# A gated mix of linear attention and a one-token FFN: gate/up in four batches of eight pieces, and kv times wo on the full TensorE array

## The chip, the cores and the metric

The kernel runs on one core of one Trainium2 chip. The metric is the device time of the whole program in microseconds (us), smaller is better; a version is measured by the median of several executions. The engines of the core are named as in the profile: PE (TensorE, matrix multiply; PEld is its weight load), DVE (VectorE), ACT (ScalarE), POOL (GpSimd) and SP (SyncE, which here only issues transfers).

## The reference

2048 tokens of width 1024 go through two branches that a per-token gate mixes. Branch a is linear attention with 32 heads of width 32. Branch b is a gated FFN (width 3584) that is applied to a single token, the one with the largest router logit; all other tokens pass through unchanged.

```python
x = A_x                                             # 1 x 2048 x 1024, bf16
g = sigmoid((x * gate_w).sum(-1, keepdims=True))
# a: linear attention
q, k, v = heads(x @ wqkv)                           # 32 heads of 32
phi = lambda t: where(t > 0, t + 1, exp(t)) + 1e-6
kv = einsum("bhsd,bhse->bhde", phi(k), v)           # 32 x 32 for each head
z  = einsum("bhsd->bhd", phi(k))
o  = einsum("bhqd,bhde->bhqe", phi(q), kv) / (einsum("bhqd,bhd->bhq", phi(q), z) + 1e-6)
a  = merge(o) @ wo
# b: FFN of the one token with the largest x @ w_r
r = x @ w_r;  i = argmax(r)
y = (silu(x[i] @ w_gate) * (x[i] @ w_up)) @ w_down
b = x;  b[i] += y * sigmoid(r[i])
return g * a + (1 - g) * b
```

## The kernel before

**Three stages.** The tokens are 16 tiles of 128 (t), the width is 8 blocks of 128 (c for the contraction, g for a group of four heads), and the queries are taken in 4 blocks of 512 tokens (j). The first stage makes keys and values tile by tile and sums kv; the second makes the rest of the queries, the denominators and the product of kv and wo; the third multiplies normalised queries with that product and mixes.

*First stage* (loop from L521): for each t, four `unit_KV(t, nb)` of eight 128x512 matmuls each (keys for nb 0 and 1, values for 2 and 3), with ACT and DVE emptying the PSUM bank; one `unit_KVACC(t - 1)` of eight 128x129 matmuls that add to kv (column 129 of each group is z); and some `unit_Q(g, j)`, eight 128x512 matmuls each, `Q_PER_T` of them per tile, j by j and g by g. Work of the FFN is put in between: `ffn_step(4)` at the places in `GU_AFTER`, `down_step` by `DOWN_STEPS`. A PSUM pool of four banks (`ps_work`) serves all these units.

*FFN pieces.* The weights stream through `ffw`, a ring of `FFN_DEPTH` = 9 buffers of 512 KB. `ffn_pieces` fixes the order of the stream: 16 pieces of gate and up for the first half of the hidden width (512 columns each), then, four times, four pieces of the second half (384 columns each) and two pieces of w_down, then the rest of w_down, and last four pieces with wo, ahead of the first of which stands the copy of x to the scratch `xp` and the load of the gate logits. A piece is taken from the front of `inflight` (L490, L500) and the next one is asked for at once (`ffn_prefetch`), all on SP in one order. A gate or up piece is 4 matmuls of an M = 32 stationary operand, one for each column tile (128x32) of the array, so that four run side by side. A w_down piece is two multiply-adds on DVE, 128x1024 each. One PSUM bank (`ps_ffn`) holds gate, then up, then the transposed h (`hps`), which is made at the next step of either kind (`ffn_flush`).

*End of the first stage* (L542 to L559): `unit_Q`, the last `unit_KVACC`, `down_finish` (the FFN row, written into `xp` by a POOL transfer), `gates`, two more `unit_Q`; z is copied to `zc` and kv to `kvbd`. Then the stage's buffers are given back (`ph1.close`, L559), and the second stage's tiles (`m_sb`, `kvT`, `rdp`, `tmpb`) take their place.

*Second stage* (L637 to L650). `den_group(0)`: 16 matmuls on column tiles; ACT adds eps, DVE takes the reciprocal (3.34 us), and SP and POOL transfers spread it to `rdp`. Then the last 15 `unit_Q`. After the first, `unit_kvT` transposes the 32 head blocks with 32 matmuls of 32x32; after those numbered in `M_AFTER` (3, 6, 9, 12) comes a `unit_M(hf, nh)`: 16 matmuls of 32x32 stationary and 512 columns, one for each 32x32 tile of the array, for half of the groups and half of the output columns. Each fills four banks (`four_banks`, three of `ps_den` and `ps_ffn`), which ACT (three) and DVE (one) copy to `m_sb`. From the fifth unit on, `norm_step(1)` broadcasts a reciprocal with a DVE shuffle (`rb`) and multiplies a block of queries on POOL.

*Third stage* (loop from L653): per tile one load of `xt` from `xp`, one ACT scale to `xg`, 16 matmuls 128x512 against `m_sb`, two DVE mixes to `ot`, one store. `den_group(1)` and the other 16 norm steps stand here, `NORM_PER_T` per tile.

**What sets the order.** Tiles, buffers and semaphores are handled by a planner: it takes the program's order as the priority, estimates when each instruction can start, and puts those that it holds ready into each engine's queue; a queue then runs in order. Where `strict[0]` is true, the wrappers `pe`, `dve`, `sp` and `act` tie each instruction to the one before on its engine, so the written order holds. In most of the first stage it is off; in `den_group` and in the loop of the second stage (L640 to L649) it is on. All matmuls and DVE operations go through such a wrapper, which is why most of the profile's lines are L78; the names of the tiles tell them apart.

Of the kernel before, what the change touches and what calls it, by code (L numbers as in the profile page):

```python
# [32 lines left out]
Q_PER_T = {4: 2, 5: 1, 6: 1, 7: 2, 8: 1, 9: 1, 10: 2, 11: 1, 12: 1, 13: 1, 14: 1, 15: 0}  # L33
GU_AFTER = {(6, "end"), (7, 1), (7, "end"), (8, 1), (8, "end"), (9, "end"), (10, "end"), (11, "end")}
M_AFTER = {3: (0, 0), 6: (0, 1), 9: (1, 0), 12: (1, 1)}
DOWN_STEPS = {9: (1, 1, 1, 1), 10: (1, 1, 1, 1), 11: (1, 1, 1, 1), 12: (1, 1, 1, 1, 1), 13: (1, 1, 1, 1), 14: (1, 1, 1, 1), 15: (1, 1, 1)}
FFN_DEPTH = 9
NORM_PER_T = [3, 2, 0, 2, 2, 2, 2, 2, 2, 2, 2, 0, 0, 0, 0, 0]
# [3 lines left out]
def kernel(  # L42
# [103 lines left out]
    nc.scalar.dma_start(out=wrg_rows[8:16, :], in_=gate_w.rearrange("(c p) -> c p", p=P))  # L146
    nc.gpsimd.memset(mzc[:], 0.0)
# [220 lines left out]
    ffw = phq.enter_context(tc.tile_pool(name="ffw", bufs=FFN_DEPTH, side="right"))  # L368
# [75 lines left out]
    def wo_pieces():  # L444
        wo_v = A_wo.rearrange("(hf r c e) n -> hf r e c n", hf=2, r=4, c=4)
        for k in range(4):
            def load(k=k):
                if k == 0:
                    cp = nc.sync.dma_start(out=xp[:], in_=x2d)
                    tc.add_manual_dep(cp.ins, ffn_state["last_ld"].ins.name, NOSYNC, reason="queue order")  # L450
                    ffn_state["last_ld"] = cp
                    gate_logits()
                wt = ffw.tile([P, 2048], BF, tag="ffw")
                for r in range(4):
                    ld = nc.sync.dma_start(out=wt[32 * r : 32 * r + 32, :].rearrange("p (c n) -> p c n", c=2),
                                           in_=wo_v[k // 2, r][:, 2 * (k % 2) : 2 * (k % 2) + 2, :])
                    tc.add_manual_dep(ld.ins, ffn_state["last_ld"].ins.name, NOSYNC, reason="queue order")
                    ffn_state["last_ld"] = ld
                return wt

            yield load, None

    def ffn_pieces():
        gu, dn = gate_up(1), down_rows()
        yield from gate_up(0)
        for _ in range(4):
            yield from islice(gu, 4)
            yield from islice(dn, 2)
        yield from dn
        yield from wo_pieces()  # L470
# [4 lines left out]
    def ffn_prefetch():  # L475
        while len(inflight) < FFN_DEPTH:
            nxt = next(pieces, None)
            if nxt is None:
                return
# [161 lines left out]
    for i in range(len(q_units)):  # L641
        unit_Q(*q_units.popleft())
        if i == 0:
            unit_kvT()
# [63 lines left out]
```

## Time and profile before

| what | value |
|---|---|
| median of 3 executions | 256.62 us (256.43 to 257.25) |
| the profiled execution | 257.25 us |
| its span, first to last instruction | 255.7 us |
| busy: DVE, ACT, POOL | 147.8, 125.7, 47.0 us |
| moved by DMA | 47.72 MB, mean 187 GB/s |
| stage 1, 0 to 166.2 us: PE busy | 162.7 us of 166.2 |
| stage 2, 166.2 to 195.3 us: PE, ACT, DVE busy | 28.7, 24.4, 21.6 us of 29.1 |
| stage 3, 195.3 to 251.9 us: PE, DVE, POOL busy | 56.3, 41.4, 27.9 us of 56.6 |

The span is what the profiler sees of one execution; the time of the execution is 1.55 us longer. The stages' rows come from the view of busy time by windows. The groups that belong to what is changed:

```profile
L78 PE MATMUL ps<-wt,xs_pad 128*32 128x512 bf16 (+1 forms) x128 | 7.5, 355 | 0.0
L78 PE MATMUL pm<-wt,kvT 32*32 32x512 bf16 x64 | 1.7, 384 | 0.0
L78 PE MATMUL pt<-ident,kvbd 32*32 32x32 bf16 x32 | 0.3, 184 | 0.0
L78 ACT CAST m_sb<-pm 128x512 bf16<-128x512 f32 x12 | 6.2, 585 | 0.0
L78 DVE CAST m_sb<-pm 128x512 bf16<-128x512 f32 x4 | 2.7, 681 | 0.0
```

A row has the line, the engine and the operation, the tile written and the tiles read, the sizes and the number of instructions; then the busy time in us and the mean of one in ns; then the idle time of the engine before them. The duration of a single matmul is its latency, longer than the spacing of matmuls that follow each other, since they are pipelined.

### The profile page before, as it was taken

The numbers are of one execution on the slowest core, as the hardware profiler recorded it, in microseconds if no ns is written. First come the engines' busy times: TensorE is split into PE (matmuls) and PEld (weight loads), VectorE is DVE, ScalarE is ACT, GpSimd is POOL, SyncE is SP. The second block draws the span as 40 slices with busy tenths as digits, with TensorE's granted clock in tenths as the row PEclk, the third lists the DMA queues.
The fourth block names the chain that finished last, engine by engine and source line by source line (L and its number), as shares of the span: only waits on it lengthen the run. The fifth ranks groups of instructions, "written<-read, shape, count | busy, mean of one in ns | idle before, by whom it ended". The sixth has DMA issues, their size and how long they took to land.

```text
span 255.7 us, 3936 instructions
## 1 busy us (share of the span) xinstructions
PE 247.7 (97%) x1471; PEld 115.1 (45%) x1498; DVE 147.8 (58%) x243; ACT 125.7 (49%) x200; POOL 47.0 (18%) x94
## 2 busy tenths in 40 slices
PE   7899999999999999999999999999999999999993
PEld 3444455445444444445444444444444444444442
DVE  0046015232246349996799813584888999953442
ACT  2096334556354444645446445468889533333200
POOL 5000001010000000000000000210566779950000
PEclk9999999999999999999999999999999999999999
DMA  6999990009999999878897760030000474454122
GB/s 178 312 336 227 260 329 7 0 19 352 348 341 320 291 275 360 266 229 299 313 489 216 180 151 0 4 123 23 0 1 3 130 223 159 143 187 141 64 82 83
DMA packets 47498, 47.72 MB, mean 187 GB/s; under 512 B 18604, under 2 KB 35380, under 8 KB 47416
## 3 DMA queue, kind: packets, MB, share of 16 engines
q1 hardware_dynamic: 47192, 47.34, 60.6%
q8 instruction: 11, 0.18, 0.3%
q0 software_dynamic: 256, 0.14, 0.2%
q14 instruction: 7, 0.06, 0.1%
q10 hardware_dynamic: 32, 0.00, 0.0%
HBM read 39.34 MB, written 8.40 MB: 187 GB/s over the span
## 4 chain that ended last, share of the span: by engine, by line
PE 95%; DMA 2%; issue 1%; SPq 1%; DVE 0%
PE ps L78 86%; PE kvacc L78 3%; PE first L78 2%; DMA wkv<-in_A_wqkv_dram 2%; PE dps L78 1%; PE rps L78 1%; SPq L78 1%; PE pm L78 1%; PE yps L78 0%; DVE ot L78 0%; PE xs_ps L78 0%; PE hps L78 0%; PE pt L78 0%; PE wps L78 0%
## 5 line engine op out<-in xcount | busy, mean ns | idle before, releaser
L78 PE MATMUL ps<-wkv,xT 128*128 128x512 bf16 x465 | 107.1, 379 | 0.7
L78 PEld LDWEIGHTS <-xT 128*128 128x128 bf16 x512 | 48.8, 98 | 59.1 <-issue 4.5
L78 PE MATMUL ps<-xT,wq 128*128 128x512 bf16 x250 | 57.4, 379 | 0.6 <-issue 0.5
L78 ACT ACTIVATE u<-ps 128x512 f32<-128x512 f32 x60 | 35.9, 598 | 40.4 <-PE ps L78 37.2
L78 PE MATMUL ps<-m_sb,pq_all 128*128 128x512 bf16 (+1 forms) x259 | 55.3, 372 | 0.3
L78 ACT ACTIVATE e<-u 128x512 f32<-128x512 f32 x64 | 40.3, 630 | 2.0
L606 POOL TENSOR_TENSOR pq_all<-pq_all,rb 128x512 bf16<-128x512 bf16 x32 | 36.6, 1169 | 14.4 <-DVE rb L78 14.0
L78 PEld LDWEIGHTS <-pq_all 128*128 128x128 bf16 x264 | 25.8, 98 | 29.8 <-issue 0.4
L78 PEld LDWEIGHTS <-wq 128*128 128x128 bf16 x256 | 24.5, 98 | 30.3 <-issue 1.7
L78 DVE SCALAR_TENSOR_TENSOR pq_all<-ps,e 128x512 bf16<-128x512 f32 x32 | 22.0, 688 | 25.7 <-ACT e L78 25.6
L78 DVE SCALAR_TENSOR_TENSOR yacc<-wt,hcol,yacc 128x1024 f32<-128x1024 bf16 x27 | 34.6, 1281 | 2.2 <-DMA wt<-in_B_w_down_dram 1.7
L78 ACT CAST vt<-ps 128x512 bf16<-128x512 f32 x32 | 18.8, 588 | 34.5 <-PE ps L78 34.5
L78 DVE SCALAR_TENSOR_TENSOR ot<-ps,gate,xg 128x512 bf16<-128x512 f32 (+1 forms) x33 | 24.0, 735 | 15.0 <-PE ps L78 14.0
L78 ACT ACTIVATE xg<-xt,omg 128x1024 f32<-128x1024 bf16 x16 | 18.1, 1146 | 25.8 <-DVE ot L78 25.8
L78 DVE SCALAR_TENSOR_TENSOR pk<-ps,e 128x512 bf16<-128x512 f32 x28 | 19.2, 687 | 19.6 <-ACT e L78 19.6
L78 DVE STREAM_SHUFFLE rb<-rdp 128x512 f32<-128x512 f32 x32 | 22.8, 746 | 0.0
L206 POOL MEMSET vt<- 128x8 bf16 x16 | 1.9, 138 | 108.8 <-PE kvacc L78 108.8
L78 PEld LDWEIGHTS <-pk 128*128 128x128 bf16 x128 | 8.5, 98 | 3.3 <-issue 0.4
L78 PE MATMUL kvacc<-vt,pk 128*128 128x129 bf16 x128 | 9.7, 221 | 0.1
L78 PE MATMUL first<-wkv,xT 128*128 128x512 bf16 x31 | 7.8, 395 | 0.8 <-DMA wkv<-in_A_wqkv_dram 0.6
L78 DVE CAST r_bf<-rps 128x512 bf16<-128x512 f32 x1 | 0.7, 692 | 12.1 <-PE rps L78 12.1
L78 PE MATMUL ps<-wt,xs_pad 128*32 128x512 bf16 (+1 forms) x128 | 7.5, 355 | 0.0
(96 smaller groups left out, 78.6 us busy)
## 6 DMA issues: line engine op xcount, KB each, us to landing
wt<-in_B_w_down_dram SPq DMA_DIRECT2D x14, 512.0 KB, 5.5
wt<-in_B_w_gate_dram SPq DMA_DIRECT2D x8, 512.0 KB, 6.0
wt<-in_B_w_up_dram SPq DMA_DIRECT2D x8, 512.0 KB, 7.2
xt<-xp SPq DMA_DIRECT2D x16, 256.0 KB, 2.7
out_dram<-ot SPq DMA_DIRECT2D x15, 256.0 KB, 2.0
wt<-in_B_w_gate_dram SPq DMA_DIRECT2D x8, 384.0 KB, 5.7
wt<-in_B_w_up_dram SPq DMA_DIRECT2D x8, 384.0 KB, 6.5
wkv<-in_A_wqkv_dram SPq DMA_DIRECT2D x8, 256.0 KB, 5.6
```

Of the source, the lines that this page charges most:

```text
L78: inst = fn(*a, **k)
L206: nc.gpsimd.memset(vt_t[t][:, :, 128:129], 1.0)
L606: nc.gpsimd.tensor_tensor(sl, sl, rb[:], op=ALU.mult)
```

## The change

- **Gate and up.** `GU_AFTER` has four places instead of eight, and eight pieces are taken at each. The stream's order is 16 pieces of the first half, 2 of w_down, 8, 4 of w_down, 8, and the rest of w_down. The number of buffers stays 9; the ring moves from the pool `phq` (which lives until the end of the second stage) to `ph1` (which ends with the first).
- **wo.** It is no longer a part of that stream. After `ph1.close` one 2 MB transfer on SP brings it into a tile of its own. The copy of x to `xp` and the load of the gate logits are issued once the stream has no piece left.
- **kv times wo.** `kvbd` is multiplied with a mask of the head blocks (made by POOL memsets at the start) when it is copied out of PSUM; eight 128x128 transposes go to one bank and one DVE copy makes `kvT`; `unit_M(g)` is two matmuls on the full array, each followed by an ACT copy.
- **Order.** One `unit_Q` more stands at t = 13 and one less after `gates`; one stands between `den_group(0)` and the transposes; 14 are left for the loop, and the eight `unit_M` follow the seventh to the fourteenth. The strict order of `den_group` and of that loop is dropped. A norm step follows each unit of the loop, and `NORM_PER_T` is 2, 0, 0, then 3.

```diff
@@ -30,12 +30,11 @@
 EPS = 1e-6
 LN1EPS = math.log1p(EPS)
 N_WARM = 6
-Q_PER_T = {4: 2, 5: 1, 6: 1, 7: 2, 8: 1, 9: 1, 10: 2, 11: 1, 12: 1, 13: 1, 14: 1, 15: 0}
-GU_AFTER = {(6, "end"), (7, 1), (7, "end"), (8, 1), (8, "end"), (9, "end"), (10, "end"), (11, "end")}
-M_AFTER = {3: (0, 0), 6: (0, 1), 9: (1, 0), 12: (1, 1)}
+Q_PER_T = {4: 2, 5: 1, 6: 1, 7: 2, 8: 1, 9: 1, 10: 2, 11: 1, 12: 1, 13: 2, 14: 1, 15: 0}
+GU_AFTER = {(6, "end"), (8, 1), (9, "end"), (11, "end")}
 DOWN_STEPS = {9: (1, 1, 1, 1), 10: (1, 1, 1, 1), 11: (1, 1, 1, 1), 12: (1, 1, 1, 1, 1), 13: (1, 1, 1, 1), 14: (1, 1, 1, 1), 15: (1, 1, 1)}
 FFN_DEPTH = 9
-NORM_PER_T = [3, 2, 0, 2, 2, 2, 2, 2, 2, 2, 2, 0, 0, 0, 0, 0]
+NORM_PER_T = [2, 0, 0, 3, 3, 3, 3, 3, 3, 3, 3, 3, 3, 3, 3, 3]
 
 
 @with_exitstack
@@ -144,6 +143,10 @@
     make_identity(nc, ident[:])
     nc.scalar.dma_start(out=wrg_rows[0:8, :], in_=B_w_r.rearrange("(c p) -> c p", p=P))
     nc.scalar.dma_start(out=wrg_rows[8:16, :], in_=gate_w.rearrange("(c p) -> c p", p=P))
+    mask_bd = const.tile([P, P], F32)
+    nc.gpsimd.memset(mask_bd[:], 0.0)
+    for i in range(4):
+        nc.gpsimd.memset(mask_bd[32 * i : 32 * i + 32, 32 * i : 32 * i + 32], 1.0)
     nc.gpsimd.memset(mzc[:], 0.0)
     for hh in range(4):
         for g0 in range(4):
@@ -365,7 +368,7 @@
         act.activation(sig[:], xs_ps[:, KC : KC + 1], ACTF.Exp, scale=-1.0)
         dve.tensor_scalar_add(sig[:], sig[:], 1.0)
         dve.reciprocal(sig[:], sig[:])
-    ffw = phq.enter_context(tc.tile_pool(name="ffw", bufs=FFN_DEPTH, side="right"))
+    ffw = ph1.enter_context(tc.tile_pool(name="ffw", bufs=FFN_DEPTH))
     h_bf = [rt.tile([P, 512], BF, name=f"h_bf{i}") for i in range(2)]
     sg_t = [rt.tile([P, 512], F32, name=f"sg{i}") for i in range(2)]
     ffn_state = {}
@@ -441,41 +444,27 @@
 
             yield load, compute
 
-    def wo_pieces():
-        wo_v = A_wo.rearrange("(hf r c e) n -> hf r e c n", hf=2, r=4, c=4)
-        for k in range(4):
-            def load(k=k):
-                if k == 0:
+    def ffn_pieces():
+        gu, dn = gate_up(1), down_rows()
+        yield from gate_up(0)
+        for n in (2, 4):
+            yield from islice(dn, n)
+            yield from islice(gu, 8)
+        yield from dn
+
+    pieces = ffn_pieces()
+    inflight = deque()
+
+    def ffn_prefetch():
+        while len(inflight) < FFN_DEPTH:
+            nxt = next(pieces, None)
+            if nxt is None:
+                if not ffn_state.get("copied"):
+                    ffn_state["copied"] = True
                     cp = nc.sync.dma_start(out=xp[:], in_=x2d)
                     tc.add_manual_dep(cp.ins, ffn_state["last_ld"].ins.name, NOSYNC, reason="queue order")
                     ffn_state["last_ld"] = cp
                     gate_logits()
-                wt = ffw.tile([P, 2048], BF, tag="ffw")
-                for r in range(4):
-                    ld = nc.sync.dma_start(out=wt[32 * r : 32 * r + 32, :].rearrange("p (c n) -> p c n", c=2),
-                                           in_=wo_v[k // 2, r][:, 2 * (k % 2) : 2 * (k % 2) + 2, :])
-                    tc.add_manual_dep(ld.ins, ffn_state["last_ld"].ins.name, NOSYNC, reason="queue order")
-                    ffn_state["last_ld"] = ld
-                return wt
-
-            yield load, None
-
-    def ffn_pieces():
-        gu, dn = gate_up(1), down_rows()
-        yield from gate_up(0)
-        for _ in range(4):
-            yield from islice(gu, 4)
-            yield from islice(dn, 2)
-        yield from dn
-        yield from wo_pieces()
-
-    pieces = ffn_pieces()
-    inflight = deque()
-
-    def ffn_prefetch():
-        while len(inflight) < FFN_DEPTH:
-            nxt = next(pieces, None)
-            if nxt is None:
                 return
             inflight.append((nxt[0](), nxt[1]))
 
@@ -524,7 +513,7 @@
             if nb == 1 and t > 4:
                 unit_KVACC(t - 1)
             if (t, nb) in GU_AFTER:
-                ffn_step(4)
+                ffn_step(8)
             steps = DOWN_STEPS.get(t, ())
             if nb < len(steps):
                 down_step(steps[nb])
@@ -538,12 +527,11 @@
         if t == 5:
             router_part2()
         if (t, "end") in GU_AFTER:
-            ffn_step(4)
+            ffn_step(8)
     unit_Q(*q_units.popleft())
     unit_KVACC(NT - 1)
     down_finish()
     gates()
-    unit_Q(*q_units.popleft())
     unit_Q(*q_units.popleft())
 
     zcol = keep.tile([P, NG], F32)
@@ -555,13 +543,15 @@
     for i in range(3):
         n = 3 if i < 2 else 2
         acc3 = kvacc[i][:, 0 : 129 * n].rearrange("p (g e) -> p g e", e=129)
-        dve.tensor_copy(kvbd[:, 3 * i : 3 * i + n, :], acc3[:, :, 0:128])
+        dve.tensor_tensor(kvbd[:, 3 * i : 3 * i + n, :], acc3[:, :, 0:128],
+                                mask_bd[:].unsqueeze(1).to_broadcast([P, n, P]), op=ALU.mult)
     ph1.close()
 
     pb = ctx.enter_context(tc.tile_pool(name="pb", bufs=1))
     m_sb = pb.tile([P, NG, D], BF)
-    wo = list(inflight)
-    kvT = pb.tile([P, 2, 4, 32], BF)
+    wo = pb.tile([P, NG, D], BF)
+    nc.sync.dma_start(out=wo[:], in_=A_wo.rearrange("(g p) n -> p g n", p=P))
+    kvT = pb.tile([P, NG, P], BF)
     rdp = [pb.tile([P, 512], F32, name=f"rdp{i}") for i in range(2)]
     for r in rdp:
         nc.gpsimd.memset(r[:], 1.0)
@@ -570,7 +560,6 @@
 
     def den_group(pair):
         dps = ps_den.tile([P, 512], F32, tag="d")
-        strict[0] = True
         for g0 in range(4):
             for jj in range(2):
                 for g1 in range(2):
@@ -579,7 +568,6 @@
                     q = 2 * jj + g1
                     pe.matmul(dps[32 * q : 32 * q + 32, :], lhsT=zc[:, g, :], rhs=pq_all[:, g, 512 * j : 512 * j + 512],
                                      start=(g0 == 0), stop=(g0 == 3), tile_position=(0, 32 * q))
-        strict[0] = False
         dn = tmpb.tile([P, 512], F32, tag="dn")
         act.activation(dn[:], dps[:], ACTF.Identity, bias=eps_t[:, 0:1])
         rd = tmpb.tile([P, 512], F32, tag="rd")
@@ -605,48 +593,32 @@
             sl = pq_all[:, g, 512 * j : 512 * j + 512]
             nc.gpsimd.tensor_tensor(sl, sl, rb[:], op=ALU.mult)
 
-    def four_banks(name):
-        banks = [ps_den.tile([P, 512], F32, tag="d", name=f"{name}{r}") for r in range(3)]
-        banks.append(ps_ffn.tile([P, 512], F32, tag="f", name=f"{name}3"))
-        return banks
-
-    def unit_kvT():
-        pt = four_banks("pt")
-        for hf in range(2):
-            for r in range(4):
-                for c in range(4):
-                    pe.matmul(pt[c][32 * r : 32 * r + 32, 32 * hf : 32 * hf + 32],
-                              lhsT=kvbd[32 * c : 32 * c + 32, 4 * hf + r, 32 * c : 32 * c + 32],
-                              rhs=ident[32 * c : 32 * c + 32, 32 * c : 32 * c + 32],
-                              start=True, stop=True, tile_position=(32 * c, 32 * r))
-        for c in range(4):
-            eng = dve.tensor_copy if c % 2 else act.copy
-            eng(kvT[:, :, c, :], pt[c][:, 0:64].rearrange("p (h d) -> p h d", h=2))
-
-    def unit_M(hf, nh):
-        pm = four_banks("pm")
-        for c in range(4):
-            for r in range(4):
-                pe.matmul(pm[r][32 * c : 32 * c + 32, :], lhsT=kvT[32 * r : 32 * r + 32, hf, c, :],
-                          rhs=wo[2 * hf + c // 2][0][32 * r : 32 * r + 32, 1024 * (c % 2) + 512 * nh : 1024 * (c % 2) + 512 * nh + 512],
-                          start=True, stop=True, tile_position=(32 * r, 32 * c))
-        for r in range(4):
-            eng = dve.tensor_copy if r == 3 else act.copy
-            eng(m_sb[:, 4 * hf + r, 512 * nh : 512 * nh + 512], pm[r][:])
+    def unit_M(g):
+        for nh in range(2):
+            ps = ps_den.tile([P, 512], F32, tag="d")
+            pe.matmul(ps[:], lhsT=kvT[:, g, :], rhs=wo[:, g, 512 * nh : 512 * nh + 512], start=True, stop=True)
+            act.copy(m_sb[:, g, 512 * nh : 512 * nh + 512], ps[:])
 
     rdA = den_group(0)
+    unit_Q(*q_units.popleft())
+    pt = ps_den.tile([P, NG, P], BF, tag="d")
+    for g in range(NG):
+        pe.transpose(pt[:, g, :], kvbd[:, g, :], ident[:])
+    dve.tensor_copy(kvT[:], pt[:])
     normalise(rdA, 0)
     normalise(rdA, 1)
-    strict[0] = True
-    for i in range(len(q_units)):
+    g_m = 0
+    nq_done = 0
+    while q_units:
         unit_Q(*q_units.popleft())
-        if i == 0:
-            unit_kvT()
-        if i in M_AFTER:
-            unit_M(*M_AFTER[i])
-        if i >= 4:
-            norm_step(1)
-    strict[0] = False
+        nq_done += 1
+        if g_m < NG and nq_done > 6:
+            unit_M(g_m)
+            g_m += 1
+        norm_step(1)
+    while g_m < NG:
+        unit_M(g_m)
+        g_m += 1
     phq.close()
 
     fin = ctx.enter_context(tc.tile_pool(name="fin", bufs=3))
```

## The prediction

> **What bounds the kernel now.** I read the page from the top: the busy time of each engine and the 40 slices, then the chain that ended last, then the groups, and last the timeline of TensorE (PE) and the SyncE (SP) transfer issues around each place that the change touches.
>
> ```profile
> span 255.7 us, 3936 instructions
> PE 247.7 (97%) x1471; PEld 115.1 (45%) x1498; DVE 147.8 (58%) x243; ACT 125.7 (49%) x200; POOL 47.0 (18%) x94
> PE   7899999999999999999999999999999999999993
> PEclk9999999999999999999999999999999999999999
> PE 95%; DMA 2%; issue 1%; SPq 1%; DVE 0%
> ...
> L78 ACT ACTIVATE u<-ps 128x512 f32<-128x512 f32 x60 | 35.9, 598 | 40.4 <-PE ps L78 37.2
> L78 ACT ACTIVATE e<-u 128x512 f32<-128x512 f32 x64 | 40.3, 630 | 2.0
> ```
>
> PE is busy from the second slice to the last but one, at the full granted clock, and 95% of the chain lies on it. So there is no stage in which another engine sets the pace: each microsecond of PE work put in or taken out, and each wait on PE, should show one for one. All other engines matter only through such waits.
>
> **The prices on PE**, from its timeline (start, busy time, what, how many):
>
> ```profile
> 66.42 1.89 PE L78 MATMUL ps<-xT,wq 128*128 128x512 bf16 x8
> 68.24 1.05 PE L78 MATMUL ps<-wt,xs_pad 128*32 128x512 bf16 x16
> 69.22 3.63 PE L78 MATMUL ps<-wkv,xT 128*128 128x512 bf16 x15
> ...
> 106.81 0.63 PE L78 MATMUL kvacc<-vt,pk 128*128 128x129 bf16 x8
> 107.28 3.62 PE L78 MATMUL ps<-wkv,xT 128*128 128x512 bf16 x16
> 110.74 3.62 PE L78 MATMUL ps<-xT,wq 128*128 128x512 bf16 x16
> ...
> 180.19 0.43 PE L78 MATMUL pm<-wt,kvT 32*32 32x512 bf16 x16
> 180.56 5.35 PE L78 MATMUL ps<-xT,wq 128*128 128x512 bf16 x23
> 185.84 0.43 PE L78 MATMUL pm<-wt,kvT 32*32 32x512 bf16 x16
> 186.21 5.35 PE L78 MATMUL ps<-xT,wq 128*128 128x512 bf16 x24
> ```
>
> Busy times overlap, so only differences of starts are prices. A 128x512 matmul: 16 from 107.28 to 110.74, 3.46/16 = 0.216 us; a unit of eight is 1.73. A gate/up batch of four pieces: 69.22 - 66.42 = 2.80, less one unit, 1.07. Its 16 matmuls run four at a time on column tiles, so the work is 4 x 0.216 = 0.86, and **0.21 us is the price of going into column tiles and back**. The 384-wide batches give the same: 0.86 against 4 x 0.162 = 0.65. One unit_M: 186.21 - 180.56 = 5.65, less 24 matmuls (5.18), 0.47. unit_kvT: from 167.20 to 174.91 stand 32 matmuls (6.91), one unit_M and it; 7.71 - 6.91 - 0.47 = 0.33.
>
> **The change, part by part.**
>
> 1. *kv times wo.* Gone: 4 x 0.47 + 0.33 = 2.21. New: 16 full matmuls of 512 columns, 16 x 0.216 = 3.46, and eight 128x128 transposes. For these the least is the spacing of kvacc (0.47 for eight 128x129, 106.81 to 107.28) and the most that of the transposes at the start, eight from 7.68 to 8.36, 0.68; I take 0.68, the same operation. **+1.93** (bounds +1.72, +1.93). Here a rule speaks against the change. The Trainium skill (TensorE: Matmul & The Clock Gate, Part 3, measured speedup) gives 10.6 times for sixteen 32x32 tiles; as an estimate that is 16 x 0.216/10.6 = 0.33 for a unit_M, where the trace has 0.47 with the switch of modes. By the page the part would cost +2.5; the measured row decides.
>
> 2. *Gate/up in four batches.* The matmuls stay; four pairs of mode switches go: 4 x 0.21, **-0.84**.
>
> 3. *The first batch needs its eighth piece sooner.* Now the first batch eats four pieces at 68.24 and the next four at 73.25. Single issues, and their microseconds from issue to landing, of the seventh and the ninth load:
>
> ```profile
> 60.12 1.29 SPq L382 DMA_DIRECT2D wt<-in_B_w_gate_dram  x1
> 62.81 1.62 SPq L382 DMA_DIRECT2D wt<-in_B_w_up_dram  x1
> ...
> wt<-in_B_w_gate_dram SPq DMA_DIRECT2D x1, 512.0 KB, 9.4
> wt<-in_B_w_up_dram SPq DMA_DIRECT2D x1, 512.0 KB, 9.7
> 118.03 1.28 DVE L78 SCALAR_TENSOR_TENSOR yacc<-wt,hcol,yacc 128x1024 f32<-128x1024 bf16 x1 [1.66 <-DMA wt<-in_B_w_down_dram]
> ```
>
> They land at 69.5 and 72.5, the eighth between them at 71.0. Nothing ahead of 68.24 changes, so the batch starts there, is through seven pieces at 68.24 + 7 x 0.216 = 69.75, and waits **1.25 us**. It costs nothing only if the planner, which puts instructions into each engine's queue by its own estimate of readiness, sets key/value matmuls of token tile 7 before the last piece (then about 0.2 for one more switch: the lower bound). It can: at 92.52 two such matmuls stand between the h transposes and a batch. But the last row, VectorE (DVE) held 1.66 us by a weight piece, shows that it counts on transfers sooner than they land; I take 1.25. Queued behind the waiting matmul is all of PE; ScalarE (ACT) and DVE only have less to do meanwhile. The later batches are fed: the second starts at 71.3 + 14.8 = 86.1 (six units, two kvacc groups, two more units), its last piece lands near 83; the third near 102.5 needs the piece that takes the first down piece's buffer, free about 2.3 us after the h columns (92.69 to 94.97 now), so near 97.5, plus 3.8 to land, 101.3; the fourth has some 4 us. Zero for these.
>
> 4. *ScalarE while wo is multiplied.* Now ACT copies 12 of 16 m_sb parts, DVE 4, spread over 10 units. After, ACT copies all 16 (589 ns each) in the last eight units: 0.60 + 0.63 + 2 x 0.59 = 2.41 us against 8 x 0.216 + 2 x 0.216 = 2.16 on PE. From the end of the first of these units, ACT has the copy of (g 7, left half) done at 8 x 2.41 - 0.59 = 18.7; PE would want it at 7 x 2.16 + 0.43 + 7 x 0.216 = 17.1. Up to **1.6 us** of wait at the first output tile, or before it on the three PSUM buffers. Down to 0.1 if the planner foresees it and runs the right half's seven ready matmuls (1.51) in between. The row at 92.52 speaks for the low end, the row at 118.03 for the high; I take 0.8. The ordering lists of the old loop, which kept two units behind the last unit_M, are gone, so this cover is gone too.
>
> 5. *wo by its own transfer.* It waits on SP until the first stage's buffers are free, about 165.3 (where xt is issued now). A 2048 KB load (wq) took 8.3 us, so it lands by 174; the first unit_M comes after den (0.98), one unit, the transposes and seven units, at 166.2 + 1.0 + 1.7 + 0.7 + 12.1 = 181.7. Zero; without these 8 us of cover, one for one. Behind it on SP stand the xt loads, wanted at 195, and the rdp rows, issued at 171.6. If those land at 175.6 instead of 174.2, the broadcasts hold DVE while PE has four buffers, 5 us of units. The Trainium skill (DMA: Bandwidth & Descriptors, Issuing engines are not separate DMA queues) says that the half issued by GpSimd shares the same 16 DMA engines; by it both halves come later and the sum stays, since the cover is the same. No row here shows the two together. The sixteen 128 KB loads of before, off the path, vanish; the copy of x moves behind seven down pieces, to land near 150 (141 now), wanted at 162.
>
> 6. *Small things.* Five memsets on an idle GpSimd; the mask product in place of a copy, 0.1 us each on DVE, behind zc; the den matmuls lose their fixed order but keep their inputs; three broadcasts per output tile instead of two: now DVE is busy 14.00 of 14 us from 209 to 223 and PE does not stop. Zero.
>
> **Sum**: 1.93 - 0.84 + 1.25 + 0.8 = **+3.1 us**. The profiled execution took 257.25 (span 255.7 and 1.55 around it), so 260.4 like for like; the median shown, 256.62, is 0.63 lower: **259.7**.
>
> **Rivals.** *Both waits hidden* (17%): the planner fills them. Then 1.72 to 1.93, less 0.84, plus 0.2 and 0.1: 1.2 to 1.4, **257.9**. For it the row at 92.52, against it the one at 118.03.
> *The loosened order breaks up the den matmuls* (17%): the 16 run four abreast in 0.98; if the planner lets other matmuls in between, they cost up to 16 x 0.216 = 3.46, +2.5 for one group, **262.2**. Likeliest in the second group, at the first output tile, where part 4 leaves PE waiting and its inputs come one unit at a time. Against it: all 16 stand side by side now, but by that very order.
> *The switches cost more than I read* (7%), so it is faster: the weight loads show 0.42 us of idle at the entry and at the exit of each batch, 0.84 together. If PE really lost that, four batches would give back 3.4, and 1.93 - 3.36 = -1.4 with the waits hidden, **255.2**. It decides from 1.93/4 = 0.48 per batch; the starts say 0.21.
> *It does not do what it says*: a batch is split by the planner. That is the first rival with more switches, 257.9 to 258.5; counted there.
>
> **How the numbers follow.** The forecast has 56%, on its own range 258.7 to 261.2 (part 3 and 4 at either end); 3% is left for no net change. The range goes down past the first rival and up past the den case: 257.4 to 262.4. A measurement of this kernel tells 0.3% (0.77 us) from no change, so "same" is 255.9 to 257.4: the 3% and the low flank of the first rival, 0.09; faster 0.06; slower 0.85.
>
> **What would show it.** Right: four runs of 32 column-tile matmuls, a gap of about 1.2 us on PE near 70 ended by the landing of a gate piece; 16 matmuls into m_sb of 0.216 each; ACT busy without pause in the last 17 us of the query units, and PE waiting on an m_sb copy at the first output tile. Wrong: den matmuls apart from each other; PE waiting on wo or on a DVE broadcast; PE's busy time lower than before; a stall at the third batch.

## The result, and the profile after

The changed kernel takes **265.76 us** (median of 4 runs, 264.72 to 267.13); the kernel before, run beside it, 256.58. The ratio is 1.0356, with a 95% interval of 1.0302 to 1.041: slower by 9.2 us, where 3.1 were forecast, and beyond the range's top of 262.4. The profiled execution took 265.26 us, its span is 263.7: 8.0 more than the span before. From the page of the changed kernel, the rows that answer to those of before:

```profile
span 263.7 us, 3784 instructions
PE 251.4 (95%) x1400; PEld 117.4 (45%) x1426; DVE 145.3 (55%) x238; ACT 126.9 (48%) x202; POOL 47.0 (18%) x99
PE   7899999999689999999989999999999999999994
PEclk9999999999959999999999999999999999999999
PE 84%; DMA 8%; SPq 3%; DVE 3%; issue 1%; ACT 0%; DVEq 0%; POOLq 0%
L77 PE MATMUL ps<-wt,xs_pad 128*32 128x512 bf16 (+1 forms) x128 | 8.0, 368 | 3.4 <-DMA wt<-in_B_w_gate_dram 3.4
```

PE is no longer busy throughout. Slices 11 and 12 show a 6 and an 8, and in slice 12 the granted clock (the share of full speed that TensorE was given) is at 0.5; a lower 8 stands near slice 21. The chain of waits has 8% on transfers and 3% on SP where it had 2% and 1%, and the gate/up group has 3.4 us of idle time ahead of it, ended by gate pieces, where it had none. (The helpers' line is now L77.) So most of the loss sits in one place. The timeline of PE around the first batch of eight (start, busy time, what, how many, and the idle time before):

```profile
67.89 1.05 PE L77 MATMUL ps<-wt,xs_pad 128*32 128x512 bf16 x16
69.20 0.40 PE L77 MATMUL ps<-wt,xs_pad 128*32 128x512 bf16 x4 [0.27 <-DMA wt<-in_B_w_gate_dram]
70.70 0.40 PE L77 MATMUL ps<-wt,xs_pad 128*32 128x512 bf16 x4 [1.10 <-DMA wt<-in_B_w_gate_dram]
72.21 0.62 PE L77 MATMUL ps<-wt,xs_pad 128*32 128x512 bf16 x4 [1.10 <-DMA wt<-in_B_w_gate_dram]
73.72 0.62 PE L77 MATMUL ps<-wt,xs_pad 128*32 128x512 bf16 x4 [0.90 <-DMA wt<-in_B_w_gate_dram]
74.27 0.61 PE L77 MATMUL ps<-wkv,xT 128*128 128x512 bf16 x1
75.10 5.06 PE L77 MATMUL ps<-wkv,xT 128*128 128x512 bf16 x14 [0.22 <-issue]
80.00 0.64 PE L77 MATMUL kvacc<-vt,pk 128*128 128x129 bf16 x8
...
91.40 1.91 PE L77 MATMUL ps<-wt,xs_pad 128*32 128x512 bf16 x32
93.24 3.63 PE L77 MATMUL ps<-wkv,xT 128*128 128x512 bf16 x15
```

The batch waits for four pieces, not one. They come 1.5 us apart and the last lands at 73.7, not at 71.0. The batch takes 6.38 us (67.89 to 74.27); one whose pieces are all there takes 1.84 (the second, 91.40 to 93.24). Then the two units of keys behind it take 5.73 us (74.27 to 80.00), where 16 such matmuls take 3.46. Why, the view of busy time by windows shows (window, length, busy us of PE, PEld, DVE, ACT and POOL, granted clock, DMA share, GB/s):

```profile
70.00:72.00 2.00, 0.40 (x4) 0.10 (x4) 0.00 (x0) 0.00 (x0) 0.00 (x0) 1.00 1.09 347
72.00:74.00 2.00, 0.90 (x8) 0.22 (x7) 0.00 (x0) 0.00 (x0) 0.00 (x0) 0.52 1.10 349
74.00:76.00 2.00, 1.78 (x8) 0.63 (x6) 0.95 (x2) 0.60 (x1) 0.00 (x0) 0.50 1.09 347
76.00:78.00 2.00, 2.00 (x6) 0.71 (x5) 2.00 (x1) 0.10 (x1) 0.00 (x0) 0.50 1.10 349
78.00:80.00 2.00, 2.00 (x9) 0.79 (x7) 1.64 (x3) 1.13 (x2) 0.00 (x0) 0.78 1.09 348
```

From about 72.1 to 78.9 the clock is granted at half (worked out from the windows that are partly at 1.0). In 76 to 78 PE is busy all the time, and the view counts six matmuls, where nine would fit at 0.216. The transfers run at 347 to 349 GB/s throughout: the stream is at its pace, PE is ahead of it.

A second stall is later. On DVE of the changed kernel:

```profile
126.11 0.68 DVE L77 SCALAR_TENSOR_TENSOR pk<-ps,e 128x512 bf16<-128x512 f32 x1
129.83 2.61 DVE L77 SCALAR_TENSOR_TENSOR yacc<-wt,hcol,yacc 128x1024 f32<-128x1024 bf16 x2 [3.03 <-DMA wt<-in_B_w_down_dram]
132.35 0.68 DVE L77 SCALAR_TENSOR_TENSOR pq_all<-ps,e 128x512 bf16<-128x512 f32 x1
132.95 0.55 DVE L77 TENSOR_TENSOR h_bf<-ps,sg 128x384 bf16<-128x384 f32 x1
```

and on its PE:

```profile
130.60 1.90 PE L77 MATMUL ps<-wkv,xT 128*128 128x512 bf16 x8
133.56 0.23 PE L77 MATMUL hps<-sel,h_bf 128*128 128x4 bf16 x3 [1.06 <-DVE h_bf L77]
```

DVE is held for 3.03 us by the first of the last eight down pieces. Its buffer had come free only when the piece ahead was consumed, its load was issued at 126.22 and landed at 129.7. Behind it in DVE's queue stand the next h, and behind h the transposes on PE, which wait 1.06 us.

**The 8.0 us of the two spans**, from differences of starts on PE: the beginning -0.35 (the first transfer lands sooner); the first batch 6.38 - 1.84, +4.5; half clock behind it 5.73 - 3.46, +2.3; the wait for h +1.2 with what follows it; four pairs of mode switches fewer, -0.84; the second stage +1.7; the end behind the last matmul 3.4 instead of 3.8 us, -0.45. Sum +8.1.

The second stage itself is as foreseen, but for the wait on ACT, which does not come. Two rows of PE and then five of ACT, from the stretch where wo is multiplied:

```profile
201.22 0.59 PE L77 MATMUL ps<-wo,kvT 128*128 128x512 bf16 x2
201.66 1.89 PE L77 MATMUL ps<-xT,wq 128*128 128x512 bf16 x8
```

```profile
197.11 0.60 ACT L77 ACTIVATE u<-ps 128x512 f32<-128x512 f32 x1
197.60 0.58 ACT L77 CAST m_sb<-ps 128x512 bf16<-128x512 f32 x1
198.06 0.64 ACT L77 ACTIVATE e<-u 128x512 f32<-128x512 f32 x1
198.60 0.59 ACT L77 CAST m_sb<-ps 128x512 bf16<-128x512 f32 x1
199.26 0.60 ACT L77 ACTIVATE u<-ps 128x512 f32<-128x512 f32 x1
```

A pair of wo matmuls costs 0.44 (201.22 to 201.66), no mode switch in it. ACT does its four instructions in 2.15 us, 197.11 to 199.26, the pace of PE (0.43 + 1.73): they start 0.46 to 0.66 apart although each lasts about 0.6. PE waits for no copy.

### The profile page after: what moved, and what is told of

It is laid out like the page before. It is cut to its first block, busy times and chain, and to the rows that moved or that the text cites. A ratio compares the mean times of both kernels' runs of the same rounds, so it can differ in the third digit from the quotient of the medians.

```text
span 263.7 us, 3784 instructions
## 1 busy us (share of the span) xinstructions
PE 251.4 (95%) x1400; PEld 117.4 (45%) x1426; DVE 145.3 (55%) x238; ACT 126.9 (48%) x202; POOL 47.0 (18%) x99
## 4 chain that ended last, share of the span: by engine, by line
PE 84%; DMA 8%; SPq 3%; DVE 3%; issue 1%; ACT 0%; DVEq 0%; POOLq 0%
PE ps L77 77%; DMA wt<-in_B_w_gate_dram 3%; SPq L385 3%; PE kvacc L77 3%; PE first L77 2%; DMA wkv<-in_A_wqkv_dram 2%; DVE yacc L77 2%; DMA wt<-in_B_w_down_dram 1%; DMA xsel<-in_A_x_dram 1%; PE dps L77 1%; PE rps L77 1%; SPq L77 1%; DVE pq_all L77 0%; ACT u L77 0%; DVE pk L77 0%
## 5 line engine op out<-in xcount | busy, mean ns | idle before, releaser
L77 PE MATMUL ps<-wkv,xT 128*128 128x512 bf16 x467 | 109.4, 384 | 0.9 <-issue 0.2
L77 PEld LDWEIGHTS <-xT 128*128 128x128 bf16 x512 | 49.5, 99 | 60.7 <-issue 6.3
L77 PE MATMUL ps<-xT,wq 128*128 128x512 bf16 x249 | 58.3, 379 | 0.5 <-issue 0.2
L77 ACT ACTIVATE u<-ps 128x512 f32<-128x512 f32 x60 | 35.8, 596 | 41.8 <-PE ps L77 41.3
L77 PE MATMUL ps<-m_sb,pq_all 128*128 128x512 bf16 (+1 forms) x259 | 55.2, 372 | 0.4 <-issue 0.2
L77 ACT ACTIVATE e<-u 128x512 f32<-128x512 f32 x64 | 40.4, 631 | 1.7
L77 DVE SCALAR_TENSOR_TENSOR pq_all<-ps,e 128x512 bf16<-128x512 f32 x32 | 21.7, 685 | 33.4 <-ACT e L77 33.4
L77 PEld LDWEIGHTS <-pq_all 128*128 128x128 bf16 x264 | 25.8, 98 | 29.8 <-issue 0.4
L77 PEld LDWEIGHTS <-wq 128*128 128x128 bf16 x256 | 24.9, 98 | 30.3 <-issue 0.8
L594 POOL TENSOR_TENSOR pq_all<-pq_all,rb 128x512 bf16<-128x512 bf16 x32 | 36.0, 1162 | 7.7 <-DVE rb L77 7.7
L77 DVE SCALAR_TENSOR_TENSOR yacc<-wt,hcol,yacc 128x1024 f32<-128x1024 bf16 x27 | 34.6, 1281 | 3.8 <-DMA wt<-in_B_w_down_dram 3.4
L77 ACT CAST vt<-ps 128x512 bf16<-128x512 f32 x32 | 18.8, 588 | 35.1 <-PE ps L77 35.1
L77 DVE SCALAR_TENSOR_TENSOR ot<-ps,gate,xg 128x512 bf16<-128x512 f32 (+1 forms) x33 | 23.9, 728 | 17.0 <-PE ps L77 16.0
L77 ACT ACTIVATE xg<-xt,omg 128x1024 f32<-128x1024 bf16 x16 | 18.2, 1148 | 25.9 <-DVE ot L77 25.9
L77 DVE SCALAR_TENSOR_TENSOR pk<-ps,e 128x512 bf16<-128x512 f32 x28 | 19.2, 687 | 15.8 <-ACT e L77 15.8
L77 DVE STREAM_SHUFFLE rb<-rdp 128x512 f32<-128x512 f32 x32 | 22.5, 743 | 0.0
L77 PE MATMUL ps<-wt,xs_pad 128*32 128x512 bf16 (+1 forms) x128 | 8.0, 368 | 3.4 <-DMA wt<-in_B_w_gate_dram 3.4
L77 PEld LDWEIGHTS <-pk 128*128 128x128 bf16 x128 | 8.5, 98 | 3.3 <-issue 0.4
L77 PE MATMUL kvacc<-vt,pk 128*128 128x129 bf16 x128 | 9.7, 221 | 0.0
L77 ACT CAST m_sb<-ps 128x512 bf16<-128x512 f32 x16 | 9.3, 583 | 0.0
L77 PE MATMUL first<-wkv,xT 128*128 128x512 bf16 x31 | 7.3, 379 | 1.6 <-DMA wkv<-in_A_wqkv_dram 1.4
```

The lines of the kernel that those rows point to most:

```text
L77: inst = fn(*a, **k)
L594: nc.gpsimd.tensor_tensor(sl, sl, rb[:], op=ALU.mult)
```

## The experiments

Ten kernels, in three groups; each group has its own runs of the kernel before, with medians of 256.36 (e1 to e4), 256.61 (e5 to e8) and 256.51 us (e9 and e10). The theory: the first batch of eight outruns the stream, the stream also starts late, and the wait costs the clock. The rivals: the second stage is to blame; or one of the three does all.

**e1: the mask memsets on another engine.** The stream of the changed kernel starts at 57.53, not 55.30, as its row numbers come from a fetch that POOL issues at 54.43, not 52.60. Is that the five new memsets on POOL?

```diff
-    nc.gpsimd.memset(mask_bd[:], 0.0)
+    nc.vector.memset(mask_bd[:], 0.0)
     for i in range(4):
-        nc.gpsimd.memset(mask_bd[32 * i : 32 * i + 32, 32 * i : 32 * i + 32], 1.0)
+        nc.vector.memset(mask_bd[32 * i : 32 * i + 32, 32 * i : 32 * i + 32], 1.0)
```

> The changed kernel with one edit: the five memsets that make the head mask at the start are done on VectorE instead of GpSimd, so that GpSimd's instruction stream is as long as in the kernel before. PE's order is that of the changed kernel. Theory 'late stream': GpSimd reads its next block of instructions just ahead of the fetch of the selected row when five instructions more stand in front of it; the weight stream waits for that row. Expected then: first gate load issued at about 55 us instead of 57.5, eighth piece landed near 71 instead of 73.7, PE's wait at the first batch about 1.6 us, no drop of the granted clock, total near 260. Rival 'the ring's new place or the traffic delays the stream': first load still at 57.5, wait and clock as in the changed kernel, total 265 to 266.

Measured: 261.44 us (261.04 to 263.34), ratio 1.0212 (1.0164 to 1.026). POOL's timeline, of the changed kernel and then of e1:

```profile
54.43 0.49 POOL L357 DMA_DIRECT2D xsel_row<-in_A_x_dram  x1 [13.30 <-issue]
```

```profile
52.01 0.49 POOL L357 DMA_DIRECT2D xsel_row<-in_A_x_dram  x1 [11.13 <-DVE pq_all L77]
```

With the memsets elsewhere the fetch starts 1.6 us after DVE has made the row's index (50.41), and with them 3.8 us after it (50.66), 2.2 us later, ended by nothing that the profile shows ("issue"). The view of transfers has a read of instructions (queue 14) at 52 to 53 in the changed kernel, ahead of this fetch, and at 53 to 54 in the kernel before, behind it. That it is POOL's read is inferred; the view doesn't name the engine. On PE of e1:

```profile
69.26 0.40 PE L77 MATMUL ps<-wt,xs_pad 128*32 128x512 bf16 x4 [0.36 <-DMA wt<-in_B_w_gate_dram]
70.77 0.40 PE L77 MATMUL ps<-wt,xs_pad 128*32 128x512 bf16 x4 [1.11 <-DMA wt<-in_B_w_gate_dram]
72.27 0.40 PE L77 MATMUL ps<-wt,xs_pad 128*32 128x512 bf16 x4 [1.09 <-DMA wt<-in_B_w_gate_dram]
72.60 3.63 PE L77 MATMUL ps<-wkv,xT 128*128 128x512 bf16 x15
```

The batch takes 4.96 us (67.64 to 72.60), the clock stays, the units behind it take 3.46. (One of the four executions, 263.34 us, had a mean clock of 0.993.) The median is above the expected 260: the batch is 3.1 us longer than one that is fed, not 1.6, as the eighth piece lands at 72.2 though the stream starts at 54.72. A table of all twelve traces shows how the starts and the pace differ (start of the row fetch on POOL, start of the weight stream on SP, time on SP from the issue of the first piece to that of the ninth; us):

| kernel | mask memsets on POOL | row fetch | stream | eight pieces |
|---|---|---|---|---|
| before | no | 52.60 | 55.30 | 7.5 |
| after | yes | 54.43 | 57.53 | 8.7 |
| e1 | no | 52.01 | 54.72 | 9.1 |
| e2, e3 | yes | 54.36, 54.14 | 57.30, 57.23 | 9.3, 9.2 |
| e4 | yes | 54.30 | 56.61 | 9.5 |
| e5 | no | 52.30 | 55.17 | 8.7 |
| e6, e7 | yes | 54.00, 54.39 | 56.90, 56.86 | 8.3, 9.7 |
| e8, e9, e10 | no | 51.65, 51.77, 51.62 | 54.42, 54.54, 54.46 | 8.4, 8.4, 8.2 |

The fetch is at 54.0 to 54.4 in all six kernels with the memsets on POOL and at 51.6 to 52.6 in all six without. And the 7.5 us in the one trace of before, from which the eighth landing was read, are the lowest of twelve. From the start of the stream to the matmuls of the eighth piece it takes 16.2 us in the changed kernel, 17.5 to 17.6 in e5 and e1; the prediction's reading, 55.30 to 71.0, is 15.7.

**e4: the memsets alone, in the kernel before.**

```diff
+    mask_bd = const.tile([P, P], F32)
+    nc.gpsimd.memset(mask_bd[:], 0.0)
+    for i in range(4):
+        nc.gpsimd.memset(mask_bd[32 * i : 32 * i + 32, 32 * i : 32 * i + 32], 1.0)
     nc.gpsimd.memset(mzc[:], 0.0)
```

> The kernel before with the five mask memsets of the changed kernel put in at the start on GpSimd, their result unused. Theory 'late stream': the row fetch is issued about 1.8 us later and the weight stream starts near 57.5 us instead of 55.3; with batches of four the fourth piece still lands before it is used (near 66 to 67 against 68.9), so the time stays 256.6. Rival 'position of the instructions has nothing to do with it': the stream starts at 55.3, time 256.6 as well; the issue times tell the two apart.

Measured: 257.15 us (256.59 to 257.93), ratio 1.0031 (1.0018 to 1.0045). The fetch is late as in the changed kernel (the stream starts at 56.61, not near 57.5):

```profile
54.30 0.49 POOL L358 DMA_DIRECT2D xsel_row<-in_A_x_dram  x1 [13.20 <-issue]
```

So the memsets by themselves make the delay. PE waits for no piece: with batches of four the stream has slack. The median is 0.8 us up all the same; the profiled execution (span 255.3) shows no place for it, and this stays open.

**e2: only the first batch cut in two.** A later stream is harmless if the second four pieces are wanted later.

```diff
-GU_AFTER = {(6, "end"), (8, 1), (9, "end"), (11, "end")}
+GU_AFTER = {(6, "end"): 4, (7, 1): 4, (8, 1): 8, (9, "end"): 8, (11, "end"): 8}
...
-                ffn_step(8)
+                ffn_step(GU_AFTER[(t, nb)])
...
-            ffn_step(8)
+            ffn_step(GU_AFTER[(t, "end")])
```

> The changed kernel with its first gate batch cut in two of four pieces, at the places that the kernel before has for them (end of tile 6, and tile 7 after the second unit); the other three batches stay at eight. Theory 'the first batch outruns the stream': the wait near 70 us and the drop of the granted clock behind it go, one pair of mode switches (0.21 us) comes back: 6.8 - 0.2 = 6.6 us less than the changed kernel, about 259. Rival 'the batches of eight wait wherever they stand': a like wait at the second batch near 85 to 90 us, total above 262. Either way the wait of 1.2 us for the transposed h behind the fourth batch stays.

Measured: 259.3 us (258.67 to 260.09), ratio 1.011 (1.008 to 1.0141), as expected. The stream starts at 57.30, the second four wait 0.53 us for the last piece, the clock stays at 1.0. One batch cut in two takes away 6.2 of the 9.2 us ((265.76 - 256.58) - (259.3 - 256.36)). The wait for h is still there, 1.41 us.

**e3: the changed second stage with the FFN of before.**

```diff
-GU_AFTER = {(6, "end"), (8, 1), (9, "end"), (11, "end")}
+GU_AFTER = {(6, "end"), (7, 1), (7, "end"), (8, 1), (8, "end"), (9, "end"), (10, "end"), (11, "end")}
...
-        for n in (2, 4):
-            yield from islice(dn, n)
-            yield from islice(gu, 8)
+        for _ in range(4):
+            yield from islice(gu, 4)
+            yield from islice(dn, 2)
...
-                ffn_step(8)
+                ffn_step(4)
...
-            ffn_step(8)
+            ffn_step(4)
```

> The changed kernel with the gate/up batches, and the order of the weight stream, of the kernel before (eight batches of four, two down pieces after each of the last four). What is left of the change is wo by its own transfer, kv times wo on the full array, and the loosened order. Theory: only PE work is left, 3.5 + 0.45 - 2.2 = +1.7 us, total 258.2 to 258.6, no drop of the clock. Rival 'ScalarE or wo is late in the second stage': PE idle before or at the first output tile, total 259.5 or more. Rival 'the late row fetch alone hurts': a wait at the first batch of four, over 260.

Measured: 257.86 us (257.42 to 259.45), ratio 1.0065 (1.0039 to 1.0091), 0.3 below the expected range. All that is not the FFN's batches costs 1.5 us, of it 0.42 for the one wait for a piece in its trace (at 73.94), in the second batch of four. PE waits for no copy and no load in the second stage. So the second stage accounts for little of the 9.2 us.

**e5: only the FFN batches, in the kernel before.** The same edit of `GU_AFTER`, `ffn_step` and the stream's order that e3 takes back, in the kernel before; nothing else.

> The kernel before with nothing changed but the gate/up batches (four of eight pieces, at the changed kernel's places) and the order of the weight stream; wo, the 32x32 tiles and the strict order stay as before, and GpSimd's start is untouched. Theory 'the first batch outruns the stream, and a down piece holds up h': four pairs of mode switches less (-0.84), about 3 us of wait at the first batch as in the run with the mask on VectorE, 1.2 to 1.6 us of wait for h behind the fourth batch: 256.4 + 3.4 to 3.8 = 260. Rival 'the loss comes from the new kv times wo': 255.5 to 256.4.

Measured: 259.3 us (258.52 to 262.26, 5 runs), ratio 1.0078 (1.0047 to 1.0108). That is 0.7 below the 260 expected. Alone, the batches cost 2.7 us, and the rest of the change 1.5 (e3), in sum 4.2 and not 9.2: the other 5 come from the two together. e1, which takes only the late start away, gives back 4.1 of them ((265.76 - 256.58) - (261.44 - 256.36)); the last 0.9 is not accounted for. Four of the five executions were granted a mean clock of at least 0.998 and took at most 259.81 us; the profiled one, 262.26, had 0.993. Its windows (columns as above):

```profile
73.00:74.00 1.00, 1.00 (x7) 0.37 (x4) 0.25 (x1) 0.60 (x1) 0.00 (x0) 0.63 1.10 352
74.00:76.00 2.00, 2.00 (x6) 0.73 (x5) 1.97 (x2) 0.00 (x0) 0.00 (x0) 0.50 1.09 348
76.00:77.00 1.00, 1.00 (x4) 0.38 (x3) 1.00 (x1) 0.59 (x1) 0.00 (x0) 0.66 1.10 349
```

Half clock for 3.4 us here (73.3 to 76.7), after waits of 0.47, 1.12 and 1.10 us; the two units behind the batch take 5.15.

**e6: the wait filled with other matmuls.** If low activity of PE costs the clock, PE kept busy while it waits should keep it.

```diff
     def ffn_step(n):
-        for _ in range(n):
+        first_b = "filled" not in ffn_state
+        ffn_state["filled"] = True
+        if first_b:
+            strict[0] = True
+            fill = ps_work.tile([P, 512], F32, tag="w", name="fill")
+        for k in range(n):
...
+            if first_b and 3 <= k < 7:
+                for _ in range(5):
+                    pe.matmul(fill[:], lhsT=warm_w, rhs=warm_x, start=True, stop=True)
             ffn_prefetch()
+        if first_b:
+            strict[0] = False
```

> The changed kernel with 20 matmuls of constants (128x512, 0.216 us each at the full clock, 4.3 us) put into the first gate batch, five after each of its fourth to seventh pieces, where PE waits for the next piece; their result is unused. The pieces land as before, so the batch can't end sooner. Theory 'the wait also lowers the granted clock': PE stays busy, the clock stays at full speed, and the units behind the batch take 3.5 instead of 5.7 us: 2 to 3 us less than the changed kernel, near 263. Rival 'the clock has no part, the loss is the wait alone': same as the changed kernel or longer, 265.5 to 267.

Measured: 262.54 us (262.39 to 263.16), ratio 1.0229 (1.0199 to 1.0259). On its PE:

```profile
72.90 1.26 PE L77 MATMUL fill<-const-bfloat16-1.0 128*128 128x512 bf16 x5
74.09 0.40 PE L77 MATMUL ps<-wt,xs_pad 128*32 128x512 bf16 x4
74.42 3.63 PE L77 MATMUL ps<-wkv,xT 128*128 128x512 bf16 x16
77.89 0.28 PE L77 MATMUL kvacc<-vt,pk 128*128 128x129 bf16 x2
```

The batch ends at 74.42, within 0.15 us of the changed kernel's 74.27: the wait is as long. But the 16 matmuls behind it take 3.47 (74.42 to 77.89) and not 5.73. Work that nobody needs makes the kernel 3.2 us faster: 2.3 of it is the clock, and the wait for h is 0.6 shorter. This ties the half clock to PE's low activity, not to the transfers, which run at 348 to 349 GB/s here too.

**e7: e2, and h ahead of the late down piece on DVE.**

```diff
-                                dve.tensor_tensor(h_bf[half][:, 0:w], ps[:, 0:w], sg_t[half][:, 0:w], op=ALU.mult)
+                                ffn_state["h"] = dve.tensor_tensor(h_bf[half][:, 0:w], ps[:, 0:w], sg_t[half][:, 0:w], op=ALU.mult)
...
-                    dve.scalar_tensor_tensor(yacc[:], w, h1, yacc[:], op0=ALU.mult, op1=ALU.add)
+                    mac = dve.scalar_tensor_tensor(yacc[:], w, h1, yacc[:], op0=ALU.mult, op1=ALU.add)
+                    if i2 == 6 and kk == 0:
+                        tc.add_manual_dep(mac.ins, ffn_state["h"].ins.name, NOSYNC, reason="h before the next down piece")
```

> The run with the first batch cut in two (259.3), with one edge more: on VectorE the first down piece of the last eight stands behind the product that makes the second half of h, instead of ahead of it. Theory 'VectorE is held by that down piece's landing and h waits behind it': PE's wait for h (1.4 us) goes, 257.7 to 258.1. Rival 'something else on VectorE is late as well': 259 or more.

Measured: 257.66 us (256.61 to 258.26, 10 runs), ratio 1.003 (1.0012 to 1.0048). Against e2 that is 1.9 us less ((259.3 - 256.36) - (257.66 - 256.61)), of which the wait for h is 1.4 and a shorter wait for a piece 0.3 (0.26 for 0.53). DVE of e7:

```profile
125.11 0.55 DVE L77 TENSOR_TENSOR h_bf<-ps,sg 128x384 bf16<-128x384 f32 x1
125.57 2.59 DVE L77 SCALAR_TENSOR_TENSOR yacc<-wt,hcol,yacc 128x1024 f32<-128x1024 bf16 x2
```

and its PE:

```profile
124.52 1.90 PE L77 MATMUL ps<-wkv,xT 128*128 128x512 bf16 x8
126.25 0.22 PE L77 MATMUL hps<-sel,h_bf 128*128 128x4 bf16 x3
```

h is made before the piece, and its transposes follow the unit without a wait. The wait of h was one of place in a queue.

**e8: the batches of eight, the first one two key units later.** In the kernel before, with e5's edit and e7's edge:

```diff
-GU_AFTER = {(6, "end"), (8, 1), (9, "end"), (11, "end")}
+GU_AFTER = {(7, 1), (8, 1), (9, "end"), (11, "end")}
```

> The kernel before with the four batches of eight, the first one five microseconds later (tile 7, after the second unit, instead of the end of tile 6), and VectorE's edge for h; all else as before. Theory: both waits gone and four pairs of mode switches saved, 256.4 - 0.84 = 255.5. Rival 'the ring of nine holds the stream while it waits for the later batch, so the second batch is short of pieces': a wait of 1 us or more near 86 us, 256.5 or more.

Measured: 256.72 us (255.6 to 257.6, 12 runs), ratio 0.9992 (0.9972 to 1.0011): no gain; the rival held. On its PE:

```profile
83.99 1.85 PE L78 MATMUL ps<-wt,xs_pad 128*32 128x512 bf16 x28
86.90 0.40 PE L78 MATMUL ps<-wt,xs_pad 128*32 128x512 bf16 x4 [1.06 <-DMA wt<-in_B_w_up_dram]
```

The wait has moved to the second batch. A ring of nine holds one batch of eight and one piece more: while the first batch stands, the stream stands.

**e9: what is left of the change when only its gain is kept.** The kernel before, with e5's order of the stream, e2's counts (4, 4, 8, 8, 8) and e7's edge.

> The kernel before with gate/up in five batches, 4, 4, 8, 8 and 8 (the first two where it has them), and VectorE's edge for h; wo, the 32x32 tiles and the strict order as before. Theory: no wait for a piece or for h is left, three pairs of mode switches are saved, 3 x 0.21 = 0.63: 255.9 to 256.0, and PE's list of waits has no weight piece in it. Rival 'the switches are cheaper than the starts say, or the time comes back later': 256.4 to 256.6, no change.

Measured: 255.86 us (255.65 to 258.03, 12 runs), ratio 0.9984 (0.9965 to 1.0004). Its trace has no wait for a piece nor for h, and its span is 254.1. Its median is the lowest of all versions; but its interval takes in 1, and so it is not shown to be faster.

**e10: e7 with e1's edit**, the changed kernel with all three faults mended.

> The run with the first batch cut in two and the edge for h (257.7), with the head mask made on VectorE, so that the weight stream starts as early as before. It has the batches 4, 4, 8, 8, 8 like the other run of this call, and differs from it by kv times wo and the order of the second stage alone. Theory: that part is PE work and nothing else, 16 x 0.216 + 0.45 - 2.21 = 1.7 us above the other run, 257.2 to 257.7, PE without a wait between the first key unit and the end. Rival 'ScalarE, wo or the loosened order costs on top': 2.5 us or more above the other.

Measured: 257.11 us (256.67 to 258.68, 12 runs), ratio 1.0027 (1.0013 to 1.0041). From the first key unit on, PE waits for nothing longer than 0.16 us. From the start of the first kvacc (36.28, in e9 36.43) to the end of the last output matmul (251.89, in e9 250.34) e10 takes 215.61 us and e9 213.91: **+1.7** for the changed second stage. The medians are 1.25 apart, the rest lies in the start and in the end, 3.3 us behind the last matmul against 3.75.

## Why the prediction was right in its sign and wrong in its size

*Part 1, kv times wo*: right, and 0.23 too high. +1.93 forecast; in the trace eight pairs take 3.46, eight transposes 0.45 (175.74 to 176.19), less 2.21 makes 1.70, and e10 against e9 gives 1.7. The transposes run at the spacing of the kvacc rows, the lower of the two bounds, not at the 0.68 of the start.

*Part 2, the switches*: right by the traces. A batch of eight in e9 saves 0.20 us against two of four (2 x 1.07 against 1.94, from differences of starts: 71.85 to 73.39 and 83.76 to 86.17, less a kvacc group of 0.47), where 0.21 was reckoned. The medians agree: e9 saves three of the four pairs and moves by -0.65 against 0.63, though its interval takes in 1. The rival in which a switch costs 0.84 falls.

*Part 3, the first batch*: **the step that failed**. The mechanism is as told, a gap that gate pieces end, but "Nothing ahead of 68.24 changes" is false, and "waits 1.25 us" became 4.5 and then 2.3 more. By size:
- The eighth piece landed at 73.7, not 71.0. The stream starts 2.2 us later than before. The prediction's part 6 has the cause and prices it at nothing: "Five memsets on an idle GpSimd". POOL was idle in time, but its instructions, when shifted, moved the issue of a fetch on which the whole stream waits (e1, e4). Taking them away brings the eighth piece only 1.45 us forward (72.27 for 73.72, e1). The rest of the 2.7 us is the pace of the stream, which was read from the quickest of the twelve traces: there SP came to the ninth issue after 7.5 us, in eleven others after 8.2 to 9.7. Even with the memsets away the batch is 3.1 to 3.2 us longer than a fed one (e1, e5). Why the pace differs was not looked into.
- PE reached the batch 0.35 sooner, so it waited longer; that is not a loss of time.
- The price of a wait was taken as its length. In the changed kernel half clock comes with it: +2.3 (e6 takes it away and leaves the wait).

*Part 3, the later batches*, "Zero for these": right for the batches, not for what stands around them. The second to fourth cost their matmuls. But the ring that feeds them also decides when the next down piece can be loaded, and DVE meets that piece ahead of h: +1.2 (e7). The prediction quoted just such a row, DVE held 1.66 us by a down piece, as a sign of how the planner reckons, and did not ask what would stand behind it in DVE's queue after the change.

*Part 4, ACT*: mis-sized, 0.8 forecast and 0 measured. The sum of four durations, 2.41, was taken as the time that they need; starts are closer, and four fit into 2.15. The bound of 0.1 was nearer.

*Part 5, wo*: right. Zero, though later than reckoned: issued at 174.01 and landed at 183.81, wanted at 188.27, 4.5 us of cover and not 8. The den matmuls stand together in both groups (from 174.32 and from 207.36), so the rival that breaks them up falls. The rival with both waits hidden was half right: the wait at the first output tile did not come.

The sum like for like: 260.4 was forecast for the profiled execution and 265.26 came. The terms account for it: first batch +3.25 (4.5 for 1.25), clock +2.3, h +1.2, ACT -0.8, kv times wo -0.25, start and end -0.8, together +4.9.

What stays open: that the instruction read itself delays the fetch is inferred from its place beside it; shown is that the memsets move the fetch. Why the half clock comes in all four executions of the changed kernel (mean clock 0.985 to 0.986) but in one of five of e5 and, by its mean clock, one of four of e1 was not settled. PE has little to do for 5.3 us in the changed kernel (68.9 to 74.3) and for 3.7 to 3.8 in e1 and e5, so a longer stretch of that kind may make the fall likelier; no run tests the length alone. One of e9's twelve executions had 0.993 as well (258.03 us), in a kernel whose trace, of another execution, has no such wait. The 0.8 us of e4's median were not settled either.

## What to carry to other kernels

A batch that takes more pieces at once needs its last piece sooner than its first: set the last landing against PE's pace, from the slowest start of the stream that is plausible and not from one trace, and follow the stream's first issue back through every engine whose instruction stream the change lengthens, idle or not. A wait on PE can cost more than its length, since the clock may fall with it; and where a ring frees a buffer late, look on every queue that consumes from it for what stands behind the waiting piece. Where an engine is to be the bound, add up the spacing of its starts, not its durations.

## What the runs showed of the hardware that was not expected

- **Half clock without a long pause.** The clock fell to 0.5 for 6.8 us, from 72.1 on, after waits of 0.27, 1.10 and 1.10 us with four matmuls between each; the fourth wait, 0.90, came after the fall. In e5 it fell for 3.4 us after three such waits, and in e1's profile three such waits left it at 1.0: so the list of waits alone does not decide it. The Trainium skill (TensorE: Matmul & The Clock Gate, Part 1, What's actually happening) has a free-running window of about 3.4 us and half clock after an idle one; the lengths agree, one window in e5 and two here. Its advice against pauses of over some 3 us (the section on why this matters for your kernels) doesn't cover this case: no pause here was longer than 1.12 us. That little work in a window counts, and not one gap, fits this and e6; no run shows where the limit lies.
- **Five memsets on an idle engine, early in the program, moved by about 2 us a transfer issue that POOL makes after more than 11 us without work** (51.6 to 52.6 without, 54.0 to 54.4 with them).
- **ACT instructions overlap in the profile.** In the second stage of the changed kernel they start on average 0.54 us apart (2.15 over four) though each is shown with about 0.6.
- **The end behind the last matmul** is 3.3 to 3.4 us with the changed second stage and 3.75 to 3.8 with that of before. No run looked for the reason.
